# Attention scores by pairs of 64 keys, and PV on 64x32 tiles, in a fused attention and gated-FFN kernel

## The chip, the cores and the metric

One NeuronCore of a Trainium2 chip. The metric is device microseconds of one execution, the median of several. The profile is of one execution; its span runs from the first to the last instruction.

Names used below: PE is TensorE, DVE is VectorE, ACT is ScalarE, POOL is GpSimd, SP is SyncE (it issues most DMAs).

## The reference

Two layers read the same x (1 x 2048 x 512) and are mixed by a gate. A is attention in 4 segments of 512 tokens, 32 heads of 16 elements: causal softmax within the segment, plus a memory M, z that each segment reads before it adds to it. B is an FFN with 1792 hidden elements.

```python
for s in range(4):
    logits = einsum('bhqd,bhkd->bhqk', qs, ks) * scale + mask      # causal, 512 x 512
    a_dot = einsum('bhqk,bhkd->bhqd', softmax(logits), vs)
    pq = phi(qs)                                                   # x+1 if x>0 else exp(x)
    a_mem = einsum('bhld,bhde->bhle', pq, M) / (einsum('bhld,bhd->bhl', pq, z) + 1e-6)
    outs.append(g * a_mem + (1 - g) * a_dot)
    M = M + einsum('bhld,bhle->bhde', phi(ks), vs)
    z = z + phi(ks).sum(over tokens)
a = concat(outs) @ wo
b = ((x @ W_gate) * (x @ W_gate > 0) * (x @ W_up)) @ W_down
out = gate * a + (1 - gate) * b          # gate = sigmoid((x * gate_w).sum(-1))
```

All inputs and the output are bf16.

## The kernel before

**Layout.** Heads are in 4 groups G of 8. In a group, q and k lie transposed, 16 rows a head, so that a row tile of 32 partitions (there are 4, `jj`) holds two heads. PSUM is split: `psL` (4 banks) takes scores, `psA` (4 banks) everything else.

**Scores and exp.** The two heads of a row tile are told apart by masked copies of k in `kp` (L684 to L686): rows of the other head are zero. `quad` makes one load of `psL`: on each of the 4 row tiles (32x128 tiles, L765) 512 query columns against 128 keys, then one exp on ACT over 128x2048 into a slot of `E` (L773). A `full` quad takes two blocks of 128 keys of one head, from the query that is 64 past the block's first, so with widths such as 448 and 64, or 320 and 192; the triangle left in the first 64 columns of each is zeroed by an affine_select on POOL (L791). The first 64 queries of all diagonal blocks are left for `half`: one quad for two groups, 32 matmuls of 64 columns, whose 128 key rows are the first 64 keys of both heads; its masks are L809. There are 72 quads, 8 of them halves.

**PV** (`flush`) turns a group's `E` into outputs, with V and a column of ones as weights (17 columns a head). First K = 128 with 4 column tiles (128x32, L824): 32 matmuls, 2048 columns in time. Then the halves' keys on 64x32 tiles (L832), 4 column tiles in the upper and 4 in the lower 64 rows: 32 matmuls, 256 columns in time. For these, odd heads need V on the other 64 partitions: `vsh`, a DMA copy per segment (L749). Two `psA` banks are held by a visit. DVE then transposes both (L843), divides, scales by the gate (`rdg` L851, which needs `gexpT`, a DMA) and transposes to `oT`.

**Memory.** `mu` (L712) multiplies phi(k) transposed (`phik`, by DMA) with V for 128 rows and 8 heads at a time, 16 whole-array matmuls of 136 columns a segment, in two visits, for 3 segments. DVE keeps the diagonal blocks (L715), POOL adds them to `Mbd` (L717), casts to `Mbd16` (L718) and scales the ones' column (L720). `nd` reads it in the next segment (L730).

**Projections, FFN, output.** L665/L667 project q, k, v; L897 gate and up; L936 and L929 the down projection and wo, into one bank. They use the whole array (128x128).

**Order.** A planner in the kernel (`Sched`) lays out every engine's instruction stream ahead of time: it holds a cost for each operation, picks by priority among the heads of the queues (with seeded ties) and emits fixed streams with semaphore waits. PE's queues are, by priority, scores and PV, memory, projections, the output product, FFN. A quad has an earliest time, 3.2 us after the last. PV of group G is put behind the first quads of group G+1 (`gate`) and asks for free `psA` banks. Every engine works its stream in order, so that one late wait holds all that stands behind it.

Of the kernel before, what the change touches and what calls it, by code (L numbers as in the profile page):

```python
# [14 lines left out]
LAT = 60.0  # L15
PE_LAT = 175.0
# [32 lines left out]
class Epoch:  # L49
    _n = 0  # L50

    def __init__(self, cls="mid", nb=1):
        self.nb = nb
        Epoch._n += 1
        self.res = f"ACCep{Epoch._n}"
        self.bank = None
        self.readers = []
        self.cls = cls


class Op:
    __slots__ = ("engs", "eng", "fns", "occs", "lat", "reads", "writes", "name", "dma", "nbytes", "mode", "ep", "role",
                 "after", "port", "base", "preds", "stream", "idx", "start", "end", "done", "cidx", "gate", "nd")

    def __init__(self, alts, reads=(), writes=(), name="", lat=0.0, dma=False, nbytes=0, mode="f", ep=None, role=None):
# [13 lines left out]
        self.after = 0.0  # L79
        self.port = name.startswith(PORT)  # L80
# [14 lines left out]
class Sched:  # L95
# [95 lines left out]
    def pv_due(self):  # L191
        q = self.queues["pe"][self.pvq]
        while q[2] < len(q[1]) and q[1][q[2]].done:
            q[2] += 1
        if q[2] >= len(q[1]) or q[1][q[2]].gate is None:
            return False
        t = self.now["pe"] + 500.0
        return all(p.done and p.end <= t for p, _ in q[1][q[2]].preds)

    def _bank_choice(self, op, e):  # L200
        cls, nb, n = op.ep.cls, op.ep.nb, len(self.bank_ep)
        idle = [p is None or all(r.done for r in p.readers) for p in self.bank_ep]
        if cls != "att":
            held = sum(not f and p.cls == cls for f, p in zip(idle, self.bank_ep))
            if held + nb > self.CAPS.get(cls, 2) or (n - sum(idle) + nb > n - (2 if self.pv_due() else 1) if nb == 1 else sum(idle) < (2 if self.relax else 3)):
                return None
# [19 lines left out]
    def ready(self, op, e):  # L226
        t0 = self.now[e]
        t = op.after
        if op.gate is not None:
            if self.mode != "r" and not op.gate.done:  # L230
                return None
            if sum(p is None or all(r.done for r in p.readers) for p in self.bank_ep) < 2:
                return None
            t = max(t, sorted(self._bank_free(p, e) for p in self.bank_ep if p is None or all(r.done for r in p.readers))[1])
# [39 lines left out]
    def place(self, op, e, start):  # L274
        op.eng = e
        if op.ep is not None and op.role == "w" and op.ep.bank is None:
            bi, _ = self._bank_choice(op, e)
            for i in range(bi, bi + op.ep.nb):
                if self.bank_ep[i] is not None:
                    op.preds += [(r, False) for r in self.bank_ep[i].readers]  # L280
                self.bank_ep[i] = op.ep
            op.ep.bank = bi
# [122 lines left out]
def plan(S, D, F):  # L405
# [4 lines left out]
        ("qT", [128, 8, 512], BF16), ("kT", [128, 4, 512], BF16), ("kp", [128, 5, 4, 320], BF16),  # L410
# [5 lines left out]
        ("Mbd", [128, 4, 136], F32), ("Mbd16", [128, 4, 136], BF16), ("mumask", [128, 2, 136], BF16), ("mutmp", [128, 2, 136], F32),  # L416
        ("braw", [128, 32], BF16), ("eb", [128, 32], F32), ("romgh", [128, 32], F32), ("epsv", [128, 32], F32),
        ("gexp", [128, NT], F32), ("omg", [128, NT], F32), ("gexpT", [128, NT * 4], F32), ("gwb", [128, 512], BF16),  ("gl", [128, NT], F32),
        ("rden", [128, 32], F32), ("rdg", [128, 32], F32), ("rdm", [128, 128], F32), ("pm8", [128, 8], F32), ("pm", [128, 2], F32), ("pmb", [128, 64], BF16), ("ident", [128, 128], BF16),
# [3 lines left out]
def build_kernel(nc, A_x, A_wq, A_wk, A_wv, A_wo, A_beta, W_g, W_u, W_d, gate_w, out):  # L423
# [5 lines left out]
    sc = Sched(seeds=(715,715,715,5226,37223,297,89,590))  # L429
# [14 lines left out]
def program(sc, nc, T, PL, PA, A_x, A_wq, A_wk, A_wv, A_wo, A_beta, W_g, W_u, W_d, gate_w, out, NSEG, KT, NF, NT, EPS, SCALE):  # L444
# [83 lines left out]
    st = []  # L528
# [8 lines left out]
    for G in range(2):  # L537
        mv = V.mumask[:, G, :].rearrange("q (h c) -> q h c", c=17)
        st.append(pool(lambda e, mv=mv: e.tensor_copy(mv, V.pm8[:, :].unsqueeze(2).to_broadcast([128, 8, 17])), 400, reads=["pm8"], writes=[f"mumask{G}"], name="mm0"))
    st.append(pool(lambda e: e.memset(V.Mbd[:], 0.0), 700, writes=["Mbd"], name="mbd0"))  # L540
    sc.queue(1, st)
# [5 lines left out]
    ds.append(dve(lambda e: e.tensor_copy(V.pmb[:], V.pm[:, 0:1].to_broadcast([128, 64])), 220, reads=["pm"], writes=["pmb"], name="pmb"))  # L547
    sc.queue(0, ds)

# [54 lines left out]
    sc.queue(1, [t for t in cst if t.eng == "dve"])  # L604

# [47 lines left out]
    def proj(s):  # L653
# [19 lines left out]
        for G in range(4):  # L673
# [8 lines left out]
            kv = V.kT[:, G, :].rearrange("q (j k) -> q j k", j=4)  # L682
            for p, o, w in ((0, 0, 128), (1, 192, 128), (2, 128, 64)):
                km = lambda e, kv=kv, p=p, o=o, w=w, ks=ks: e.tensor_scalar(V.kp[:, ks, :, o:o + w], kv[:, :, 0:w], V.pm[:, p % 2:p % 2 + 1], None, ALU.mult)  # L684
                kq = lambda e, kv=kv, ks=ks: e.tensor_tensor(V.kp[:, ks, :, 128:192], kv[:, :, 0:64], V.pmb[:, :].unsqueeze(1).to_broadcast([128, 4, 64]), ALU.mult)
                ka = lambda e, kv=kv, p=p, o=o, w=w, ks=ks: e.activation(V.kp[:, ks, :, o:o + w], kv[:, :, 0:w], ACT.Copy, scale=V.pm[:, p % 2:p % 2 + 1])  # L686
                evs.append(sc.add(Op([("dve", km, 350 if w == 128 else 285)] + ([("act", ka, 720 if w == 128 else 500)] if s else []) + ([("pool", kq, 650)] if p == 2 and s else []), reads=[f"kT{G}", "pm"], writes=[f"kp{ks}_{p}"], name=f"kmask{s}_{G}_{p}")))
# [15 lines left out]
    def mu(s):  # L703
        pes, ds, ps = [], [], []
        for hf in range(2):
            ep = Epoch()

            def fn(e, hf=hf, ep=ep):
                for g in range(2):
                    G = 2 * hf + g  # L710
                    for tt in range(4):
                        ins = e.matmul(A(ep)[:, g * 136:(g + 1) * 136], lhsT=V.phik[:, tt, G * 128:(G + 1) * 128], rhs=V.vaug[:, s % 2, tt, 8 * G:8 * G + 8, :].rearrange("q h c -> q (h c)"), start=(tt == 0), stop=(tt == 3))  # L712
                return ins
            pes.append(pe(fn, mm(136, 8), reads=[f"phik{2 * hf}", f"phik{2 * hf + 1}"] + va(s), name=f"mu{s}_{hf}", ep=ep, role="w"))
            ds.append(dve(lambda e, ep=ep: e.tensor_tensor(V.mutmp[:, :, :], A(ep)[:, 0:272].rearrange("q (g c) -> q g c", g=2), V.mumask[:, :, :], ALU.mult), t_dve(272), reads=["mumask0", "mumask1"], writes=["mutmp"], name=f"mum{s}_{hf}", ep=ep, role="r"))  # L715
            Mh = V.Mbd[:, 2 * hf:2 * hf + 2, :]
            ps.append(pool(lambda e, Mh=Mh: e.tensor_tensor(Mh, Mh, V.mutmp[:, :, :], ALU.add), t_pool(272, 2.2), reads=["mutmp", "Mbd"], writes=["Mbd"], name=f"mua{s}_{hf}"))  # L717
        ps.append(pool(lambda e: e.tensor_copy(V.Mbd16[:], V.Mbd[:]), t_pool(544, 1.2), reads=["Mbd"], writes=["Mbd16"], name=f"mu16_{s}"))  # L718
        dc = lambda t: t[:, :, :].rearrange("q g (h c) -> q g h c", c=17)[:, :, :, 16]
        ps.append(pool(lambda e: e.tensor_tensor(dc(V.Mbd16), dc(V.Mbd), V.eb[:, :].rearrange("q (g h) -> q g h", g=4), ALU.mult), 230, reads=["Mbd", "Mbd16", "reb"], writes=["Mbd16"], name=f"mu16_{s}"))  # L720
        return pes, ds, ps

    def nd(s):
        pes, ds, sps = [], [], []
        for i in range(4):
# [9 lines left out]
            pes.append(pe(fnum, mm(136, 4), reads=[f"phiq{G}" for G in range(4)] + ["Mbd16"], name=f"num{s}_{i}", ep=ep, role="w"))  # L735
# [12 lines left out]
    def vsh_dma(s):  # L748
        Q["spv"].append(dma("sp", lambda e: e.dma_start(V.vsh[64:128, :, :, :].rearrange("q t h c -> q (t h c)"), V.vaug[0:64, s % 2, :, :, :].rearrange("q t h c -> q (t h c)")), 1 << 17, occ=700.0, reads=va(s), writes=["vsh"], name=f"vsh{s}"))  # L749
# [3 lines left out]
    def att(s, between):  # L753
        pes, acts, pools, ds, pvs = [], [], [], [], []

        def quad(tag, parts, slot=None):
            e = slot
# [4 lines left out]
            def fq(q, parts=parts):  # L762
                for (kap, _, qs, q0, o, w) in parts:
                    for jj in range(4):
                        ins = q.matmul(PL[:, jj, o:o + w], lhsT=kap(jj), rhs=V.qT[32 * jj:32 * jj + 32, qs, q0:q0 + w], start=True, stop=True, tile_position=(32 * jj, 0), skip_group_check=True)  # L765
                return ins
            rd = sorted({k for (_, ks, _, _, _, _) in parts for k in ks} | {f"qT{qs}" for (_, _, qs, _, _, _) in parts})
            np_ = len(parts)
            pes.append(pe(fq, sum(w for (_, _, _, _, _, w) in parts) / 2.4 + 10.0 + 3.0 * (np_ - 1), reads=rd, writes=[f"bankL{b}" for b in range(4)], name=f"quad{s}_{tag}", mode="r"))
            pes[-1].after = 12000.0 + 3200.0 * qctr[0]  # L770
            qctr[0] += 1
            eout = V.E[:, e, :, :] if slot is None else V.E[:, e, :, :].rearrange("q h c -> q (h c)").rearrange("q (g h c) -> q h g c", g=2, c=256)
            acts.append(act(lambda a, eout=eout: a.activation(eout, PL[:, :, :] if slot is None else PL[:, :, :].rearrange("q h (g c) -> q h g c", g=2), ACT.Exp, scale=SCALE), t_act(2048), reads=[f"bankL{b}" for b in range(4)], writes=[f"E{e}"], name=f"exp{s}_{tag}"))  # L773
            return e

        def keys(n, j):
            ks, o = kslot(s, n // 2), 192 * (n % 2)
            return lambda jj: V.kp[32 * jj:32 * jj + 32, ks, j, o:o + 128], [f"kp{ks}_{n % 2}"], qslot(s, n // 2)

        def full(tag, n, blocks):  # L780
            o, parts, regs = 0, [], []
            for j in blocks:
                w = 448 - 128 * j
                parts.append((*keys(n, j), 128 * j + 64, o, w))
                regs.append(o)
                o += w
            assert o == 512
            e = quad(tag, parts)
            for o in regs:
# [264 lines left out]
```

## Time and profile before

| | |
|---|---|
| median of 3 runs | 269.09 us (268.21 to 269.18) |
| profiled execution, span | 266.3 us |
| PE busy | 262.3 us, 2860 matmuls |
| DVE, ACT, POOL busy | 186.9, 186.8, 112.1 us |
| scores L765 | 768 matmuls, 28.7 us busy |
| PV L824 | 512 matmuls, 16.8 us busy |
| DMA | 18.13 MB, queue q1 busy 26.9% |

How to read it: a matmul's length in the trace has its drain in it, so that the lengths of one group overlap; the pace is seen from start to start. The page's rows have the line, the engine, the operation, out<-in, the shape and count; behind the bar the busy time, the mean of one in ns, and the idle time before them with what ended it. The timeline has start, length and instructions, merged where they follow each other.

### The profile page before, as it was taken

Reading aid. Unit: us, or ns where it says so; the run is one execution under the profiler, and the core shown is the slowest. Engines: PE = TensorE matmul, PEld = TensorE weight load, DVE = VectorE, ACT = ScalarE, POOL = GpSimd, SP = SyncE. Lnnn points to the kernel's source line nnn. Section 1 sums busy time; section 2 is a strip of 40 time slices with the busy share of each in tenths; the row PEclk is TensorE's granted clock in tenths of the full one; section 3 lists DMA queues with packets and bytes.
Section 4 is the critical chain, followed back from the end, with each engine's and each line's share of the span. In section 5 each row is a group of like instructions: output and inputs, shape, how many; then the busy total and the mean of one; then the engine's idle time right before and its main releaser. Section 6 shows DMA issues by size and latency. Waiting matters only on the chain.

```text
span 266.3 us, 6827 instructions
## 1 busy us (share of the span) xinstructions
PE 262.3 (98%) x2860; PEld 116.6 (44%) x2860; DVE 186.9 (70%) x370; ACT 186.8 (70%) x165; POOL 112.1 (42%) x227
## 2 busy tenths in 40 slices
PE   7999999999999999999999999999999999999996
PEld 3444444444444444444344444444444444434444
DVE  5788878888876699887868677757763556585500
ACT  3698899798896596886877687677866566774021
POOL 3025654475529343575367233822282225521000
PEclk9999999999999999999999999999999999999999
DMA  6899635921221325120022131000212000000011
GB/s 183 226 385 184 117 78 103 338 59 23 59 44 25 82 60 81 39 42 4 0 64 46 35 99 26 23 2 0 56 28 61 20 22 22 0 2 2 1 39 41
DMA packets 34209, 18.13 MB, mean 68 GB/s; under 512 B 23937, under 2 KB 33922, under 8 KB 34178
## 3 DMA queue, kind: packets, MB, share of 16 engines
q1 hardware_dynamic: 34048, 17.69, 26.9%
q8 instruction: 22, 0.36, 0.6%
q14 instruction: 9, 0.07, 0.1%
q10 hardware_dynamic: 130, 0.01, 0.0%
HBM read 9.75 MB, written 2.11 MB: 45 GB/s over the span
## 4 chain that ended last, share of the span: by engine, by line
PE 97%; DMA 1%; SPq 0%; issue 0%; ACT 0%; DVE 0%; DVEq 0%
PE psA L897 38%; PE psA L936 19%; PE psA L667 11%; PE psL L765 9%; PE psA L824 6%; PE psA L665 6%; PE psA L929 5%; PE psA L832 1%; PE psA L730 1%; PE psA L712 1%; DMA hT<-in_A_x_dram 1%; SPq L480 0%; ACT xT L578 0%; DVE osb L945 0%; PE psL L587 0%
## 5 line engine op out<-in xcount | busy, mean ns | idle before, releaser
L773 ACT ACTIVATE E<-psL 128x2048 bf16<-128x2048 f32 x72 | 135.0, 1875 | 37.7 <-PE psL L765 36.1
L791 POOL TENSOR_SCALAR_AFFINE_SELECT E<-E 128x256 bf16<-128x256 bf16 x128 | 51.8, 428 | 99.8 <-ACT E L773 91.0
L897 PE MATMUL psA<-xT,wu 128*128 128x512 bf16 x224 | 59.6, 380 | 0.0
L897 PE MATMUL psA<-xT,wg 128*128 128x512 bf16 x224 | 59.4, 380 | 0.0
L936 PE MATMUL psA<-wd,hT 128*128 128x512 bf16 (+2 forms) x238 | 54.1, 367 | 0.0
L809 POOL TENSOR_SCALAR_AFFINE_SELECT E<-E 64x512 bf16<-64x512 bf16 (+1 forms) x64 | 43.4, 703 | 23.8 <-ACT E L773 13.7
L908 DVE TENSOR_TENSOR hT<-psA,rl 128x512 bf16<-128x512 f32 x56 | 38.4, 686 | 14.6 <-PE psA L897 13.6
L843 DVE STREAM_TRANSPOSE Tn<-psA 128x512 f32<-128x512 f32 x32 | 21.2, 696 | 21.7 <-PE psA L832 21.6
L905 ACT ACTIVATE rl<-psA 128x512 bf16<-128x512 f32 x36 | 21.5, 597 | 14.9 <-PE psA L897 11.6
L897 PEld LDWEIGHTS psA<-xT,wg 128*128 128x128 bf16 x224 | 20.7, 98 | 24.8 <-issue 1.9
L936 PEld LDWEIGHTS psA<-wd,hT 128*128 128x128 bf16 x238 | 21.4, 98 | 22.7 <-issue 1.5
L897 PEld LDWEIGHTS psA<-xT,wu 128*128 128x128 bf16 x224 | 20.2, 98 | 24.2 <-issue 2.3
L765 PE MATMUL psL<-qT,kp 32*128 32x64 bf16 (+3 forms) x768 | 28.7, 245 | 0.0
L765 PEld LDWEIGHTS psL<-qT,kp 32*128 32x128 bf16 x768 | 9.9, 92 | 30.2 <-issue 18.2
L945 DVE TENSOR_SCALAR osb<-psA,omg 128x512 bf16<-128x512 f32 (+1 forms) x9 | 6.3, 695 | 16.7 <-PE psA L929 13.8
L906 DVE TENSOR_SCALAR rl<-psA 128x512 bf16<-128x512 f32 x20 | 13.8, 690 | 4.4 <-PE psA L897 3.6
L824 PE MATMUL psA<-E,vaug 128*17 128x192 bf16 (+3 forms) x512 | 16.8, 273 | 0.0
L667 PE MATMUL psA<-xT,wk 128*128 128x512 bf16 x64 | 16.6, 380 | 0.0
L667 PE MATMUL psA<-xT,wq 128*128 128x512 bf16 x64 | 16.3, 380 | 0.3 <-ACT xT L578 0.3
L929 PE MATMUL psA<-wo,oT 128*128 128x512 bf16 (+2 forms) x68 | 16.4, 367 | 0.0
L665 PE MATMUL psA<-wv,xT 128*128 128x512 bf16 x64 | 15.5, 380 | 0.0
L946 ACT ACTIVATE osb<-psA,omg 128x512 bf16<-128x512 f32 (+1 forms) x8 | 5.4, 673 | 14.0 <-PE psA L929 12.8
(82 smaller groups left out, 241.3 us busy)
## 6 DMA issues: line engine op xcount, KB each, us to landing
out_dram<-osb SPq DMA_DIRECT2D x15, 128.0 KB, 1.7
wg<-in_B_W_gate_dram SPq DMA_DIRECT2D x8, 224.0 KB, 5.4
wu<-in_B_W_up_dram SPq DMA_DIRECT2D x8, 224.0 KB, 5.6
wd<-in_B_W_down_dram SPq DMA_DIRECT2D x1, 1792.0 KB, 9.0
osb<-in_A_x_dram SPq DMA_DIRECT2D x12, 128.0 KB, 2.3
vsh<-vaug SPq DMA_DIRECT2D x4, 272.0 KB, 3.4
hT<-in_A_x_dram SPq DMA_DIRECT2D x4, 128.0 KB, 2.2
wq<-in_A_wq_dram SPq DMA_DIRECT2D x4, 128.0 KB, 2.4
```

The lines of the kernel that those rows point to most:

```text
L665: ins = e.matmul(A(ep)[:, :], lhsT=V.xT[:, kt, tok + col * 128:tok + (col + 1) * 128], rhs=w[:, kt, :], start=(kt == 0), stop=(kt == KT - 1))
L667: ins = e.matmul(A(ep)[:, :], lhsT=w[:, kt, col * 128:(col + 1) * 128], rhs=V.xT[:, kt, tok:tok + 512], start=(kt == 0), stop=(kt == KT - 1))
L765: ins = q.matmul(PL[:, jj, o:o + w], lhsT=kap(jj), rhs=V.qT[32 * jj:32 * jj + 32, qs, q0:q0 + w], start=True, stop=True, tile_position=(32 ...
L773: acts.append(act(lambda a, eout=eout: a.activation(eout, PL[:, :, :] if slot is None else PL[:, :, :].rearrange("q h (g c) -> q h g c", g ...
L791: pools.append(pool(lambda g, ap=ap: g.affine_select(out=ap, in_=ap, compare_op=ALU.is_ge, fill=0.0, base=64, pattern=[[0, 4], [1, 64]], c ...
L809: pools.append(pool(lambda e, ap=ap, base=base: e.affine_select(out=ap, in_=ap, compare_op=ALU.is_ge, fill=0.0, base=base, pattern=[[0, 8] ...
L824: ins = q.matmul(A(eps[p])[32 * jj:32 * jj + 17, 512 - w:512], lhsT=V.vaug[:, s % 2, j, 8 * G + 2 * jj + p, :], rhs=V.E[:, e, jj, o:o + w] ...
L897: ins = e.matmul(A(ep)[:, :], lhsT=w[:, kt, f * 128:(f + 1) * 128], rhs=V.xT[:, kt, c * 512:(c + 1) * 512], start=(kt == 0), stop=(kt == K ...
L905: evs.append(sc.add(Op([("act", lambda e, ep=eg, r=r: e.activation(V.rl[:, r, :], A(ep)[:, :], ACT.Relu), t_act(512)), ("dve", lambda e, e ...
L908: evs.append(dve(lambda e, ep=eu, r=r, hs=hs: e.tensor_tensor(V.hT[:, hs, :], A(ep)[:, :], V.rl[:, r, :], ALU.mult), t_dve(512), reads=[f" ...
L929: ins = e.matmul(A(ep)[:, 0:c1 - c0], lhsT=V.oT[:, o0 + G, i * 128:(i + 1) * 128], rhs=V.wo[:, G, c0:c1], start=st_ and G == 0, stop=sp_ a ...
L936: ins = e.matmul(A(ep)[:, 0:c1 - c0], lhsT=V.hT[:, slots[f], i * 128:(i + 1) * 128], rhs=V.wd[:, f, c0:c1], start=st_ and f == f0, stop=sp ...
```

## The change

- `kp` holds, for each of 8 chunks of 64 keys, those keys for head 0 and for head 1 of the row tile side by side: 128 weight columns. Two masked copies make it, not three. A quad's scores have head 0 on partitions 0 to 63 and head 1 on 64 to 127.
- Quads of a group: chunk 0 (512 queries); 1 and 7; 2 and 6; 3 and 5; and chunk 4 of two groups together. Each chunk has two masks on POOL, one of 64 and one of 128 partitions.
- PV of a group is one operation on 64x32 tiles: for 8 chunks, the upper 64 rows for head 0 and the lower for head 1, 64 matmuls of 512 to 64 columns. V is wanted on both halves, so two `vsh` copies a segment.
- The memory product is put ahead of PV of group 1 (`MU_G`), 64 products of 34 columns on 4 column tiles (128x32) into one bank; DVE adds it to `Mc`, and POOL spreads `Mc` into `Mbd16` by one masked product a group. The factor of the ones' column goes into `mumask` at the start.
- The planner counts how many free banks a PV visit asks for (`nbk`), and has other seeds, so the order of the other work moves too.

```diff
+MU_G = 1
...
-    sc = Sched(seeds=(715,715,715,5226,37223,297,89,590))
+    sc = Sched(seeds=(52936,98560,17166,30259,57195,44848,1710,92264))
...
-            kv = V.kT[:, G, :].rearrange("q (j k) -> q j k", j=4)
-            for p, o, w in ((0, 0, 128), (1, 192, 128), (2, 128, 64)):
...
+            kv = V.kT[:, G, :].rearrange("q (c k) -> q c k", c=8)
+            for p in range(2):
+                km = lambda e, kv=kv, p=p, ks=ks: e.tensor_scalar(V.kp[:, ks, :, 64 * p:64 * p + 64], kv, V.pm[:, p:p + 1], None, ALU.mult)
...
     def mu(s):
...
+        ep = Epoch("att")
+
+        def fn(e):
+            for G in range(4):
+                for tt in range(4):
+                    for j in range(4):
+                        ins = e.matmul(A(ep)[32 * j:32 * j + 32, 34 * G:34 * G + 34], lhsT=V.phik[:, tt, 128 * G + 32 * j:128 * G + 32 * j + 32],
+                                       rhs=V.vaug[:, s % 2, tt, 8 * G + 2 * j:8 * G + 2 * j + 2, :].rearrange("q h c -> q (h c)"),
+                                       start=(tt == 0), stop=(tt == 3), tile_position=(0, 32 * j), skip_group_check=True)
+            return ins
...
+        d = dve(lambda e: e.tensor_tensor(V.Mc[:], V.Mc[:], A(ep)[:, 0:136].rearrange("q (g c) -> q g c", g=4), ALU.add), t_dve(136), reads=["Mc"], writes=["Mc"], name=f"mum{s}", ep=ep, role="r")
+        ps = []
+        for G in range(4):
+            j3 = lambda t, G=G: t[:, G, :].rearrange("q (j c) -> q j c", c=34)
+            ps.append(pool(lambda e, G=G, j3=j3: e.tensor_tensor(j3(V.Mbd16), V.Mc[:, G, :].unsqueeze(1).to_broadcast([128, 4, 34]), j3(V.mumask), ALU.mult), t_pool(136, 2.2),
+                           reads=["Mc", "mumask"], writes=[f"Mbd16_{G}"], name=f"mu16_{s}"))
...
     def vsh_dma(s):
...
+        for u in range(2):
+            to, of = V.vsh[64 - 64 * u:128 - 64 * u], V.vaug[64 * u:64 * u + 64, s % 2]
...
         def quad(tag, parts, slot=None):
...
+                for G, c, o in parts:
                     for jj in range(4):
-                        ins = q.matmul(PL[:, jj, o:o + w], lhsT=kap(jj), rhs=V.qT[32 * jj:32 * jj + 32, qs, q0:q0 + w], start=True, stop=True, tile_position=(32 * jj, 0), skip_group_check=True)
+                        r = slice(32 * jj, 32 * jj + 32)
+                        ins = q.matmul(PL[:, jj, o:o + 512 - 64 * c], lhsT=V.kp[r, kslot(s, G), c, :], rhs=V.qT[r, qslot(s, G), 64 * c:512], start=True, stop=True, tile_position=(32 * jj, 0), skip_group_check=True)
...
+            o = [o for _, _, o in parts]
+            for i, x in enumerate(o):
                 for h, base in ((64, 0), (128, 64)):
+                    ap = V.E[0:h, e, :, x:x + 64]
+                    pools.append(pool(lambda g, ap=ap, base=base: g.affine_select(out=ap, in_=ap, compare_op=ALU.is_ge, fill=0.0, base=base, pattern=[[0, 4], [1, 64]], channel_multiplier=-1),
...
         def flush():
...
+            mem = mu(s) if G == MU_G and s < NSEG - 1 else None
...
+            def fpv(q):
+                for c in range(8):
+                    e, o = at[G, c]
+                    t, u = c // 2, c % 2
+                    for p in range(2):
+                        r = slice(64 * p, 64 * p + 64)
+                        v = V.vaug[r, s % 2, t, :, :] if u == p else V.vsh[r, t, :, :]
                         for jj in range(4):
-                            ins = q.matmul(A(eps[p])[32 * jj:32 * jj + 17, 512 - w:512], lhsT=V.vaug[:, s % 2, j, 8 * G + 2 * jj + p, :], rhs=V.E[:, e, jj, o:o + w],
-                                           start=(j == 0), stop=False, tile_position=(0, 32 * jj), skip_group_check=True)
...
+                            ins = q.matmul(A(eps[p])[32 * jj:32 * jj + 17, 64 * c:512], lhsT=v[:, 8 * G + 2 * jj + p, :], rhs=V.E[r, e, jj, o:o + 512 - 64 * c],
+                                           start=(c == 0), stop=(c == 7), tile_position=(64 * p, 32 * jj), skip_group_check=True)
+                return ins
...
         for G in range(4):
...
+            at |= quad(f"{G}A", [(G, 0, 0)])
+            at |= quad(f"{G}B", [(G, 1, 0), (G, 7, 448)])
             pair = flush()
...
             if G % 2 == 0:
-                half(f"{G}C", G)
+                at |= quad(f"{G}E", [(G, 4, 0), (G + 1, 4, 256)], slot=7)
+            at |= quad(f"{G}C", [(G, 2, 0), (G, 6, 384)])
             if pair:
                 pair[0].gate = pes[k]
...
+            at |= quad(f"{G}D", [(G, 3, 0), (G, 5, 320)])
```

## The prediction

> **What bounds the kernel now.** I read the page's busy shares first, then the chain that ended last, the waits of TensorE, and last the timeline of a few microseconds, where single visits can be priced.
>
> ```profile
> span 266.3 us, 6827 instructions
> PE 262.3 (98%) x2860; PEld 116.6 (44%) x2860; DVE 186.9 (70%) x370; ACT 186.8 (70%) x165; POOL 112.1 (42%) x227
> ...
> PEclk9999999999999999999999999999999999999999
> ...
> PE 97%; DMA 1%; SPq 0%; issue 0%; ACT 0%; DVE 0%; DVEq 0%
> ...
> L791 POOL TENSOR_SCALAR_AFFINE_SELECT E<-E 128x256 bf16<-128x256 bf16 x128 | 51.8, 428 | 99.8 <-ACT E L773 91.0
> ...
> L809 POOL TENSOR_SCALAR_AFFINE_SELECT E<-E 64x512 bf16<-64x512 bf16 (+1 forms) x64 | 43.4, 703 | 23.8 <-ACT E L773 13.7
> ...
> vsh<-vaug SPq DMA_DIRECT2D x4, 272.0 KB, 3.4
> ```
>
> TensorE is 98% busy, at full granted clock, and 97% of the chain. The view of its waits has three lines, all from the first microseconds:
>
> ```profile
> PE psL L553 <- PEq L1039: 0.8, 1, 0.8
> PE psA L667 <- ACT xT L578: 0.3, 1, 0.3
> PE psL L566 <- DMA hT<-in_A_x_dram: 0.2, 1, 0.2
> ```
>
> So after the start nothing holds TensorE up; its time is the sum of what it is given, and the question is what the change takes out of that sum. The timeline (start, length, instruction) prices it. A length includes the drain, so I take start to next start:
>
> ```profile
> 43.83 0.81 PE L897 MATMUL psA<-xT,wu 128*128 128x512 bf16 x3
> 44.48 0.59 PE L897 MATMUL psA<-xT,wg 128*128 128x512 bf16 x2
> 45.00 0.40 PE L765 MATMUL psL<-qT,kp 32*128 32x192 bf16 x8
> 45.33 1.05 PE L824 MATMUL psA<-E,vaug 128*17 128x448 bf16 x32
> 46.31 0.20 PE L832 MATMUL psA<-E,vaug 64*17 64x64 bf16 x4
> ...
> 46.42 0.20 PE L832 MATMUL psA<-E,vsh 64*17 64x64 bf16 x4
> 46.55 0.60 PE L897 MATMUL psA<-xT,wg 128*128 128x512 bf16 x2
> ...
> 48.82 0.41 PE L765 MATMUL psL<-qT,kp 32*128 32x64 bf16 x32
> 49.16 0.39 PE L897 MATMUL psA<-xT,wu 128*128 128x512 bf16 x1
> ```
> ```profile
> 62.14 0.64 PE L712 MATMUL psA<-vaug,phik 128*128 128x136 bf16 x8
> 62.61 1.03 PE L897 MATMUL psA<-xT,wu 128*128 128x512 bf16 x4
> ```
>
> Three 512-column matmuls take 0.65 us, 0.216 each: 0.417 ns a column and about 3 ns a matmul. A score quad (45.00 to 45.33) streams 512 columns on four row tiles, 0.213 us, and costs 0.33. The first part of PV (L824, 45.33 to 46.31) streams 2048, 0.853, and costs 0.98. Its second part (L832, to 46.55) streams 256 on eight 64x32 tiles, 0.107, and costs 0.24. Each change of tile shape therefore costs 0.12 to 0.13 us.
>
> **The change, part by part.** *PV.* Before, a visit is 0.98 + 0.24 = 1.22 us with two changes on leaving. After, it streams 512 + 448 + ... + 64 = 2304 columns on the eight tiles, as many as before (2048 + 256), and leaves once: 0.96 + 0.13 = 1.09; for the staggered start of eight chunks I take 1.10. Gain 0.12 x 16 visits = 1.9. No row shows this shape with wide streams. Bounds: 1.09 (gain 2.1), or the pace of L832 throughout: its eight groups of four start 0.11 us / 7 = 0.0157 apart, 0.031 for 64 columns, 0.49 ns a column, 1.26 a visit (loss 0.6). I take the first, because 0.031 is eight matmuls starting 4 ns apart, a charge per matmul that 512 columns cover.
>
> *Memory product.* Before: six visits like 62.14 to 62.61, 0.475 x 6 = 2.85, without a change of shape. After: three visits of 64 small products, 16 groups of four column tiles. The nearest row is again L832, where a tile gets new weights and a new product every 0.031: 16 x 0.031 = 0.50, plus 0.12 for one more change, 0.62; x 3 = 1.85. Gain 1.0. Bounds: four starts at 4 ns (0.016 a group, 0.37 a visit, gain 1.75), or each group as dear as a 136-column matmul (0.059, 1.07 a visit, loss 0.35).
>
> *Order and scores.* The instruction order has 177 changes of shape before and 165 after: 16 go with PV, 3 come with the memory product (both priced), which leaves one more, 0.12 lost. Quads stay 72 with the same columns; the eight made of 32 narrow matmuls (48.82 to 49.16, 0.34) become ordinary (0.33): 0.1 gained.
>
> Sum: 1.9 + 1.0 - 0.1 + 0.1 = 2.9 us. The profiled execution spans 266.3, the median of the runs shown is 269.09, so 2.8 lie around the span and I take the same 2.8 after: span 263.4, time **266.2**. All bounds together: 2.1 + 1.75 gives 265.2, -0.6 - 0.35 gives 270.0.
>
> The rest I cost at nothing, because it lies beside TensorE:
> - Masks. 256 of 128x256 or half as many partitions at 0.428 (L809's two forms, 64 and 128 partitions, take the same time) are 110 us where L791 and L809 take 95. GpSimd loses the third key mask (7.7 us) and the old memory update (L717, L718, L720: 7.7) and gets 12 products of 136 elements, by L717's 0.76 for 272 some 0.4 each, 5 us. In all 112 becomes about 116 of 266. A quad now ends with four masks: exp starts 0.45 after the quad, takes 1.875, masks 1.7, ready after 4.05. PV comes two or more quads later (72 quads, one in about 3.2 us), margin above 2. Thinnest is the last PV: 0.33 + 20 matmuls of 0.216 and a change are 4.75, margin 0.6. If a cover goes, all queued matmuls wait with PV.
> - The second shifted copy of V. Each PV now needs both copies at its start. In the first segment SP issues them behind the same four xT transposes, which end at 22.96, 0.6 each, and 3.4 to landing: 28. My count of the order puts the first PV at 31.6 (34.8 before). In later segments the copies wait only for the old PV, some 16 us earlier.
> - Moved on SP's queue: gscr and gexpT of segment 0 now stand behind both phik pairs and more xT transposes. From 24.2: phik 2.5, xT 1.3, phik 2.5, xT 3.9, gscr 0.5, xT 2.6, gexpT 3.1, 2.2 to landing: 42.8. On VectorE the rdg that needs it now stands behind the memory addition, which cannot run before 45. If gexpT came later than that, evictions behind rdg would stop TensorE.
> - The end. Before, the last PV's chain to oT takes 5.9 us from 244.0 with three hT products between. After, none stands between, so 3.7, under 22 matmuls, 4.75.
> - VectorE, ScalarE and GpSimd together lose 16 key masks (0.35 to 0.7 each); the four added copies (272 KB each, 1.1 MB of 18.1) fall on DMA queues that the page shows 27% busy.
>
> **Rivals.** (1) *Small products do not overlap.* If the 64 memory products each stand alone, a 34-column one is by the rows above 34 x 0.417 + 3 = 17 ns: 1.09 + 0.12 = 1.21 a visit, 3.6 in all, 0.8 lost where I count 1.0 gained: 268.0. Against it: L832 starts a matmul every 4 ns. 4%. The Trainium skill ("TensorEngine Tiling (Array Packing)", Instruction Overhead) says that each matmul pays about 60 cycles however narrow. As 64 separate charges of 25 ns, an estimate from that page, the visit would be 1.72 and the kernel 269.5; L832's 4 ns between starts on different tiles speak against such a reading, and only a charge per tile, 16 x 25 ns, is in keeping with them.
>
> (2) *PV stays at L832's pace* of 0.49 ns a column: 0.6 lost instead of 1.9 gained, 268.7. For it: it is the only row of this shape. Against: the charge looks per matmul. 7%.
>
> (3) *PV waits for masks.* A wait of 0.2 us at each of 16 visits takes 3.2 back: 269.4. For it: 192 masks become 256, and one engine makes them all. Against: 56% idle and the margins above. 7%; 3 of these go past 270.4, with 0.27 a visit.
>
> (4) *Slower: upper and lower rows do not stream side by side when wide.* Then a visit streams 4608 columns, 1.92 + 0.13 = 2.05 instead of 1.10: 15.2 more, 281.4. It decides once a visit costs over 1.37 (1.22 plus the 1.0 of the other parts and 1.35 of noise over 16). For it: no row has two wide streams there. Against: L832 passes eight 64-column streams in 0.031, where one after the other would need 0.053. 4%.
>
> **How the numbers follow.** The forecast has 78%. Faster by over 0.5% means below 267.75, slower above 270.4; half a per cent is about what a measurement of this kernel tells from no change. (1), (2) and the milder part of (3) fall between, 15%; the rest of (3), and (4), make 7%. The range goes from the best bounds, 265.2, less 0.4 for scatter (the three runs lie within 1.0), to rival (2) at 268.7: the forecast, (1) and (2) lie in it, so well over 8 in 10; the joint worst bound of 270.0 is left out.
>
> **What would show it.** PV groups of 64x32 tiles with 1.10 from first start to the next shape; memory visits of 0.5 to 0.65; changes of 0.12; waits of TensorE still only at the start; GpSimd near 116. Wrong would be: a visit of 1.26 or 2.05 (rivals 2, 4), a memory visit over 1.1 (rival 1), or a new wait of TensorE on masks, vsh or an eviction.

## The result and the profile after

| | before | after |
|---|---|---|
| median beside each other | 268.86 us (268.21 to 269.18, 4 runs) | 264.85 us (264.76 to 265.37, 4 runs) |
| profiled execution, span | 266.3 us | 263.0 us |
| matmul records, weight loads | 2860, 2860 | 2714, 2748 |
| DVE, ACT, POOL busy | 186.9, 186.8, 112.1 us | 181.5, 188.7, 119.5 us |

The ratio is 0.9866, with an interval of 0.9846 to 0.9886: 1.3% faster. The profiled execution of after took 264.76 us, 1.76 more than its span.

These lines of the page of after answer to those shown of before:

```profile
span 263.0 us, 6637 instructions
PE 254.4 (97%) x2714; PEld 113.1 (43%) x2748; DVE 181.5 (69%) x359; ACT 188.7 (72%) x167; POOL 119.5 (45%) x283
...
PEclk9999999999999999999999999999999999999999
...
PE 94%; issue 2%; DVE 1%; DMA 1%; SPq 0%; ACT 0%; DVEq 0%
...
L786 POOL TENSOR_SCALAR_AFFINE_SELECT E<-E 64x256 bf16<-64x256 bf16 (+1 forms) x256 | 111.8, 446 | 122.2 <-ACT E L781 100.9
```

TensorE is still the bound, at full granted clock. The chain has a new entry, "issue", with 2%, and the view of TensorE's waits names it too:

```profile
PE psA L874 <- issue: 2.1, 13, 0.2
PE psA L913 <- issue: 1.0, 6, 0.2
PE psL L556 <- PEq L1014: 0.8, 1, 0.8
...
PE psA L673 <- ACT xT L581: 0.3, 1, 0.3
PE psL L569 <- DMA hT<-in_A_x_dram: 0.2, 1, 0.2
```

The last three are the waits of the start, as before; behind the start TensorE waits for no mask, no copy of V and no eviction. The "issue" entries are read as no waits at all. There are 34 more weight loads than matmul records, where before had as many of each, and at 34 places two starts lie 0.22 us further apart than the pace, one 512-column matmul (0.216): a record is missing there, in 15 of them that of the first wide matmul after a PV visit. (Three of the holes are put down to DVE, 0.2 each.) Such a hole costs nothing, and the span bears that out: 34 real stops of 0.22 would be 7.5 us. The timeline (start, length, instruction) has a memory visit, then a PV visit followed by a hole:

```profile
105.64 0.66 PE L716 MATMUL psA<-vaug,phik 128*32 128x34 bf16 x64
106.23 0.39 PE L809 MATMUL psA<-E,vaug 64*17 64x512 bf16 x4
```
```profile
131.51 0.39 PE L809 MATMUL psA<-E,vaug 64*17 64x512 bf16 x4
...
132.48 0.20 PE L809 MATMUL psA<-E,vaug 64*17 64x64 bf16 x4
132.84 1.67 PE L671 MATMUL psA<-wv,xT 128*128 128x512 bf16 x7 [0.16 <-issue]
```

The memory visit takes 0.59 from its first start to PV's. From PV's first start to the next one shown is 1.33; less the missing matmul (L671 has 62 records for 64 weight loads) it is 1.11. The one visit that a quad follows, and all 16 in an experiment whose trace lacks no record (`old_memory_product`), give 1.100. All 16 visits of before take 1.22 (0.982 and 0.241), so the visits alone give 16 x 0.123 = 2.0 us.

### The profile page after: what moved, and what is told of

Its sections match the earlier page's. It is cut to its first block, busy times and chain, and to the rows that moved or that the text cites. A ratio compares the mean times of both kernels' runs of the same rounds, so it can differ in the third digit from the quotient of the medians.

```text
span 263.0 us, 6637 instructions
## 1 busy us (share of the span) xinstructions
PE 254.4 (97%) x2714; PEld 113.1 (43%) x2748; DVE 181.5 (69%) x359; ACT 188.7 (72%) x167; POOL 119.5 (45%) x283
## 4 chain that ended last, share of the span: by engine, by line
PE 94%; issue 2%; DVE 1%; DMA 1%; SPq 0%; ACT 0%; DVEq 0%
PE psA L874 37%; PE psA L913 19%; PE psA L673 11%; PE psL L775 9%; PE psA L809 7%; PE psA L906 5%; PE psA L671 5%; PE psA L736 1%; DMA hT<-in_A_x_dram 1%; PE psA L716 1%; DVE vaug L699 0%; SPq L484 0%; DVE phiq L657 0%; ACT xT L581 0%; DVE osb L922 0%
## 5 line engine op out<-in xcount | busy, mean ns | idle before, releaser
L786 POOL TENSOR_SCALAR_AFFINE_SELECT E<-E 64x256 bf16<-64x256 bf16 (+1 forms) x256 | 111.8, 446 | 122.2 <-ACT E L781 100.9
L874 PE MATMUL psA<-xT,wg 128*128 128x512 bf16 x212 | 57.0, 380 | 1.9 <-issue 1.6
L913 PE MATMUL psA<-wd,hT 128*128 128x512 bf16 (+2 forms) x229 | 52.2, 366 | 1.1 <-issue 1.0
L775 PE MATMUL psL<-qT,kp 32*128 32x192 bf16 (+7 forms) x512 | 28.5, 287 | 0.0
L882 ACT ACTIVATE rl<-psA 128x512 bf16<-128x512 f32 x32 | 19.1, 597 | 10.2 <-PE psA L874 9.5
L923 ACT ACTIVATE osb<-psA,omg 128x512 bf16<-128x512 f32 (+1 forms) x12 | 8.1, 679 | 17.9 <-PE psA L906 14.0
L883 DVE TENSOR_SCALAR rl<-psA 128x512 bf16<-128x512 f32 x24 | 16.7, 696 | 3.2 <-PE psA L874 2.5
L809 PE MATMUL psA<-E,vaug 64*17 64x128 bf16 (+7 forms) x512 | 18.7, 283 | 0.0
L809 PE MATMUL psA<-E,vsh 64*17 64x128 bf16 (+7 forms) x512 | 18.3, 283 | 0.0
L671 PE MATMUL psA<-wv,xT 128*128 128x512 bf16 x62 | 14.7, 380 | 0.3 <-issue 0.3
L809 PEld LDWEIGHTS psA<-E,vaug 64*17 64x17 bf16 x512 | 11.6, 86 | 6.0 <-issue 3.6
```

The costliest lines, as they stand in the source:

```text
L671: ins = e.matmul(A(ep)[:, :], lhsT=V.xT[:, kt, tok + col * 128:tok + (col + 1) * 128], rhs=w[:, kt, :], start=(kt == 0), stop=(kt == KT - 1))
L775: ins = q.matmul(PL[:, jj, o:o + 512 - 64 * c], lhsT=V.kp[r, kslot(s, G), c, :], rhs=V.qT[r, qslot(s, G), 64 * c:512], start=True, stop=Tr ...
L786: pools.append(pool(lambda g, ap=ap, base=base: g.affine_select(out=ap, in_=ap, compare_op=ALU.is_ge, fill=0.0, base=base, pattern=[[0, 4] ...
L809: ins = q.matmul(A(eps[p])[32 * jj:32 * jj + 17, 64 * c:512], lhsT=v[:, 8 * G + 2 * jj + p, :], rhs=V.E[r, e, jj, o:o + 512 - 64 * c], sta ...
L874: ins = e.matmul(A(ep)[:, :], lhsT=w[:, kt, f * 128:(f + 1) * 128], rhs=V.xT[:, kt, c * 512:(c + 1) * 512], start=(kt == 0), stop=(kt == K ...
L882: evs.append(sc.add(Op([("act", lambda e, ep=eg, r=r: e.activation(V.rl[:, r, :], A(ep)[:, :], ACT.Relu), t_act(512)), ("dve", lambda e, e ...
```

## The experiments

Two theories stood at the start. The first is the prediction's: PV visits shrink by 0.12, memory visits by 1.0 in all, and everything else hides beside TensorE, so that each part alone brings its own share. The rivals put the gain, or a loss that hides in it, elsewhere: in halves that do not really run together, in the order, in the masks. Each run has a time of the kernel before on the same chip: 268.46, 268.43 and 268.19 in the three batches.

### The halves of the array, one after the other: `pv_one_half_after_other`

```diff
             def fpv(q):
-                for c in range(8):
-                    e, o = at[G, c]
-                    t, u = c // 2, c % 2
-                    for p in range(2):
+                for p in range(2):
+                    for c in range(8):
+                        e, o = at[G, c]
+                        t, u = c // 2, c % 2
```

> The changed kernel with the two loops of PV swapped: all 8 chunks on the upper 64 rows, then all 8 on the lower, so that the two halves of the array no longer stream side by side. Same matmuls, same order of everything else. Theory (TensorE's time is the sum of its streams, and the gain of the new PV needs both halves at once): each visit streams 4608 columns instead of 2304, 0.96 us more, 16 visits, so 264.85 + 15.4 = 280.2, visits of about 2.06 us. Rival (the halves hardly overlap in the changed kernel either, and the gain came from elsewhere): within 3 us of the changed kernel.

Measured: 275.83 us in one run, span 274.1. A visit takes 1.81 instead of 1.10, and 16 x 0.71 = 11.4 is the span's loss of 11.1. So the gain does hang on the upper and the lower half streaming side by side. The expected loss was larger, though. The timeline of the first visit shows why:

```profile
32.40 0.28 PE L809 MATMUL psA<-E,vaug 64*17 64x256 bf16 x4
32.41 0.39 PE L809 MATMUL psA<-E,vsh 64*17 64x512 bf16 x8
32.59 0.40 PE L809 MATMUL psA<-E,vaug 64*17 64x128 bf16 x8
32.64 0.51 PE L809 MATMUL psA<-E,vsh 64*17 64x64 bf16 x8
```

In this kernel the 512-column products of the lower half come after all of the upper half's. Four of them start at 32.41, right behind the upper half's 256-column group, while the upper groups of 192, 128 and 64 columns, earlier in the program, start at 32.50, 32.59 and 32.64 (the first of them is merged into the second line). The idle half is fed about 0.24 us ahead of its turn, and a visit is 0.25 shorter than the 2.06 expected. The Trainium skill ("TensorE: Matmul & The Clock Gate", Part 3: Packing small matmuls) says that matmuls start and end strictly in program order; these starts differ from that, and the measurement decides.

### The two parts alone, with the seeds that were there

`old_memory_product` is the changed kernel with the memory product of before; `new_memory_product_alone` is the kernel before with the new memory product put ahead of PV of group 1. Neither gets new seeds.

In the first, besides `mu` and its masks as they were:

```diff
-            mem = mu(s) if G == MU_G and s < NSEG - 1 else None
+            mem = None
```

In the second, besides the new `mu` and `mumask`:

```diff
+            mem = mu(s) if G == MU_G and s < NSEG - 1 else None
+            if mem:
+                put(dmu=[mem[1]], poolmu=mem[2])
...
+            if mem:
+                pair.insert(0, mem[0])
```

> The changed kernel with the old memory product (16 whole-array matmuls of 136 columns a segment in two visits, the old update on VectorE and GpSimd), so the new scores and PV alone. Theory (sum of the parts): loses the memory part's 1.07 us (2.85 before, 3 x 0.594 after), and 2 changes of shape less than the changed kernel's 162 outside the memory visits give or take 0.1 each: 265.8 to 266.1, that is 2.8 to 3.1 under the kernel before. Rival (the smaller memory work on VectorE and GpSimd carries the gain): close to 268.9.

> The kernel before with only the memory product changed: 64 products of 34 columns ahead of PV of group 1, one bank, the new update. It stands next to PV's 128x32 part, so it has the same tile shape and costs no change of its own. Theory (sum): gains 2.85 - 3 x (0.594 - 0.10) = 1.37 us, 268.86 - 1.4 = 267.5; 177 changes of shape as before. Rival (planning for three free banks at one visit costs waits): no gain, and waits of TensorE ahead of the memory product.

Measured: 269.26 us, ratio 1.0039 (1.0027 to 1.0051), and 269.65 us, 1.0049 (1.0037 to 1.0061). Both missed: each part alone is slower than before. All PV visits of the first take 1.100, so the term is there, and something gives it back. The views of TensorE's waits, the first kernel's and then the second's:

```profile
PE psL L771 <- ACT E L777: 1.0, 1, 1.0
...
PE psA L870 <- DVE rl L879: 0.3, 1, 0.3
PE psA L902 <- DVE oT L830: 0.3, 1, 0.3
```
```profile
PE psL L773 <- ACT E L781: 1.2, 3, 0.8
...
PE psA L835 <- POOL E L799: 0.5, 1, 0.5
```

These are waits for an exp, a mask and evictions, in places where the plan has the work a little too close to its consumer. Before and after have none of them. The question became whether the parts or the order bring them.

### The seeds of before in the changed kernel: `old_seeds`

```diff
-    sc = Sched(seeds=(52936,98560,17166,30259,57195,44848,1710,92264))
+    sc = Sched(seeds=(715,715,715,5226,37223,297,89,590))
```

> The changed kernel with the planner's seeds of the kernel before, so another order of the same work; 165 changes of shape in both. Theory (TensorE's work sets the time, the order hardly matters as long as nothing waits): 264.9 to 266 , and any excess shows as waits of TensorE in the profile, not as dearer visits. Rival (the gain is that of a luckier order): 268 or more.

Measured: 274.07 us, ratio 1.0203 (1.0173 to 1.0232); the profiled span is 272.9, 9.9 over that of after. Missed widely. The waits, and the timeline at the longest of them:

```profile
PE psA L809 <- issue: 3.8, 1, 3.8
PE psL L775 <- ACT E L781: 1.7, 3, 1.0
```
```profile
50.36 0.20 PE L809 MATMUL psA<-E,vaug 64*17 64x64 bf16 x3
54.31 0.21 PE L809 MATMUL psA<-E,vaug 64*17 64x64 bf16 x1 [3.75 <-issue]
54.45 1.89 PE L874 MATMUL psA<-xT,wg 128*128 128x512 bf16 x4
```

TensorE stops between the third and the fourth matmul of a group, inside one operation, where nothing that the program waits for stands. After it, four matmuls take 1.7 us from start to start, 0.42 each, twice the usual. The view by windows (each engine's busy time; last three the granted clock, the DMA share and GB/s) confirms both:

```profile
50.40:54.30 3.90, 0.16 (x23) 0.03 (x4) 0.05 (x1) 0.00 (x0) 1.26 (x3) 0.77 1.51 343
54.30:59.30 5.00, 4.99 (x19) 1.48 (x18) 2.57 (x5) 2.42 (x2) 1.56 (x4) 0.50 0.89 92
```

The granted clock is 0.50 from 52.5 to 59.3 us, and TensorE works for 5.0 us of that, so the clock costs 2.5. With the stop of 3.8 and the other waits (1.7 for exps, some 1.2 more) that is 9.2 of the 9.9; the rest is not placed. Since the program has no wait inside an operation, the cause of the stop is to be looked for outside it. The trace has a DMA queue of instructions (q8, 16 KB each, one for some 260 of TensorE's records). In this kernel none of its packets runs between 34.9 and 51.5 us, with DMA at 343 GB/s from the loads of `wo` and `wd` at the end of that time; then one comes, and 2.8 us after its start TensorE resumes. In after the fetch starts at 46.2, just as those loads are issued.

### The same with the load of `wd` later: `old_seeds_late_wd`

```diff
     for t in lsp:
         t.after = 42000.0
+    lsp[-1].after = 52000.0
```

> The changed kernel with the old seeds, where TensorE stopped for 3.9 us inside a PV visit at 50.4 us and then ran 4 us at half clock, now with the 1.8 MB load of wd planned 10 us later; the order of TensorE is the same up to 60 us. Theory (the stop is an instruction fetch that stood behind that load: the fetch queue moved nothing from 33.7 to 51.5 us): no stop at 50 us, and 272 falls to 266 to 268, unless a later fetch meets the load instead. Rival (the stop has to do with the PV visit itself): it stays at 50 us.

Measured: 269.57 us, ratio 1.0046 (1.0033 to 1.0058). The stop is at the same instruction and now 1.3 us long; the granted clock stays at 1.00:

```profile
50.07 0.20 PE L810 MATMUL psA<-E,vaug 64*17 64x64 bf16 x3
51.40 0.19 PE L810 MATMUL psA<-E,vaug 64*17 64x64 bf16 x1 [1.13 <-issue]
```

The fetch comes at 49.0, behind `wo` alone, instead of 51.5, and TensorE resumes 2.4 us after its start. So moving 1.8 MB of loading out of the way cuts the stop by 2.5 us, keeps the clock and takes 4.5 us off the kernel: that this load lengthens the stop is shown. The stop did stay at 50 us, as the rival said, but the rival doesn't explain why its length follows the load. That the fetch is the link, and that `wo` makes the 1.3 us that are left, is read from the records; no run moved the fetch itself or `wo`. The time misses what was expected by these 1.3 us and by waits of 0.9, 0.7 and 0.5 at other places.

### The two parts alone, each with an order of its own

The same two kernels again, with seeds for which the planner's own plan leaves little of TensorE idle.

```diff
-    sc = Sched(seeds=(52936,98560,17166,30259,57195,44848,1710,92264))
+    sc = Sched(seeds=(72224,66228,45311,67877,42182,25599,42182,67877))
```
```diff
-    sc = Sched(seeds=(715,715,715,5226,37223,297,89,590))
+    sc = Sched(seeds=(71326,715,4683,6717,55110,55110,92428,590))
```

> The run with the old memory product again, with other planner seeds, found for this kernel so that the plan has little idle TensorE time. In the first such run TensorE waited about 2.6 us that the changed kernel does not wait. Theory (sum of the parts, and waits are a matter of the order): its matmuls and changes of shape come to 1.2 us more than the changed kernel's, so 264.85 + 1.2 = 266.0 and up to 266.6 with small waits, 2 to 2.5 under the kernel before (268.46 in the same batch). Rival (the new PV alone gains nothing, it needs the new memory product beside it): 268 or more.

> The run with the memory product alone changed again, with planner seeds found for it. Theory: 1.4 us less work for TensorE than the kernel before, so 268.46 - 1.4 = 267.1, to 267.6 with small waits. Rival (three banks at one visit cost waits whatever the order): 268.5 or more, with waits ahead of the visits of group 1.

Measured: 266.45 us, 0.9922 (0.9900 to 0.9943), and 267.33 us, 0.9956 (0.9939 to 0.9972). The first has no wait of TensorE behind the start, the second 0.6 us of them by the starts (the view of waits names 0.2). So the new scores and PV bring 268.43 - 266.45 = 2.0 us, the new memory product 1.1, and the two losses above were the order's. In the second kernel the memory visit needs no change of shape of its own, so that 1.4 was to be had, less those waits; in after it is 1.07. The sum of 3.1 stands against a gain of both of 3.3 in the profiled spans and 4.0 in the medians, or 3.6 against the median of before in the next batch (268.46).

### Masks: `masks_twice` and `masks_one_and_a_half`

The first makes every mask twice, in the same order; the second only those of 128 partitions.

```diff
+                        if op.name.startswith("mask"):
+                            op.fns[e](engobj).then_inc(self.sem["again"], 1)
+                            extra += 1
+                            engobj.wait_ge(self.sem["again"], extra)
                         res = op.fns[e](engobj)
```

In the second the condition is:

```diff
-                        if op.name.startswith("mask"):
+                        if op.name.startswith("mask") and "m64" in op.writes[0]:
```

> The changed kernel, every instruction in its order, but GpSimd makes each mask twice (same result): 256 masks become 512, busy 119.5 + 112 = 231 us, 88% of the span. Theory (the cover of the masks is 2 us or more at all PV visits and 0.6 at the last): after a quad with two chunks the masks end 0.45 + 1.9 + 3.6 = 5.9 us after its start; PV two quads later, 6.4, does not wait; only the last one, 4.75 after, waits 1.2: 264.85 + 1.2 = 266.0. Rival (the masks are nearly on the path already): waits at most of the 16 visits, 270 or more.

> The changed kernel, same order, with only the second mask of each chunk (128 partitions) made twice: 384 masks instead of 256, the same 3 for every 2. With 512 masks TensorE waited for masks at 15 places, up to 3.5 us: a quad with two chunks then brought 8 masks of 0.448, 3.6 us, and quads come every 3.2 us, so that GpSimd fell behind. Theory now (the cover is a rate): 6 masks are 2.7 us a quad, under 3.2, so no backlog; the last PV, 4.75 after its quad, waits 0.45 + 1.9 + 2.7 - 4.75 = 0.3: 265 to 266. Rival (GpSimd is already at its limit in the changed kernel, where 4 masks are 1.8): one half of the loss of the doubled run, 275 or more.

Measured: 300.41 us, ratio 1.1207 (1.1173 to 1.1242), missed by far; and 265.18 us, 0.9895 (0.9878 to 0.9913), as expected. The waits of TensorE on masks, first and second:

```profile
PE psA L814 <- POOL E L791: 21.1, 13, 3.5
PE psA L721 <- POOL E L791: 3.5, 2, 2.5
```
```profile
PE psA L814 <- POOL E L791: 0.4, 1, 0.4
```

A quad with twice its four masks needs 8 x 0.448 = 3.6 us of POOL, and a quad comes every 3.2: a backlog grows, and 13 PV visits wait for it, and two memory visits that stand directly in front of a PV: 15 of 16 places. (The rest of the loss is clock: five times it is halved for 3.41 us, of which TensorE works 16.4 in all, so 8.2 us are lost.) The view by windows shows when it is halved. The first window here has a part of the longest wait (3.46 us, from 67.07 to 70.53), the second a wait of 2.1 us, the third is what follows that. After the window stand its length and PE's busy time; the last three figures are as above.

```profile
65.46:68.87 3.41, 1.61 (x14) 0.51 (x12) 1.87 (x4) 3.41 (x4) 3.14 (x7) 1.00 0.19 51
...
273.67:277.08 3.41, 1.36 (x7) 0.39 (x5) 0.69 (x1) 0.00 (x0) 2.90 (x8) 1.00 0.01 2
277.08:280.50 3.42, 3.37 (x68) 1.68 (x69) 1.18 (x2) 0.00 (x0) 0.00 (x0) 0.50 0.02 5
```

The changes of the clock in this trace lie whole multiples of 3.41 us apart, and the windows are such steps. Where TensorE was busy for 0.5 to 1.4 us of a step, the clock was halved in the next; where it was busy for 1.6 or more, it was not. The longest wait falls into two steps and costs no clock.

Half as many extra masks, six or 2.7 us a quad, leave POOL ahead: it is busy 67%, and only the last PV waits, because behind the last exp it has no slack.

### Fewer weight columns in the memory product: `memory_half_weights`

```diff
-    ins = e.matmul(A(ep)[32 * j:32 * j + 32, 34 * G:34 * G + 34], lhsT=V.phik[:, tt, 128 * G + 32 * j:128 * G + 32 * j + 32],
+    ins = e.matmul(A(ep)[32 * j:32 * j + 16, 34 * G:34 * G + 34], lhsT=V.phik[:, tt, 128 * G + 32 * j:128 * G + 32 * j + 16],
```

> The changed kernel, same order, with memory products whose weights are 16 columns instead of 32 (it leaves out the odd heads' part of the memory). In the changed kernel the first 28 products of a visit start about 3.6 ns apart (25 ns for each four) and the rest 8.3 ns apart (33 ns for each four). Supply theory (each product is a weight load and a matmul, and TensorE's stream brings one of the two about every 4.15 ns once what it had queued is used up): nothing changes, visits of 0.59. Weight theory (the time is that of loading 32 columns): the later products come closer, visits of 0.53 or less. The kernel's time is the same within 0.2 us in both.

Measured: 265.13 us in one run; a visit takes 0.58 instead of 0.59. In both, groups of four products start 25 ns apart at first and 33 ns apart from the ninth group on, with 8 ns from each product to the next. Half the weight columns leave both paces as they are, so the width of the weights doesn't set them. That how fast loads and products are handed over sets them is the theory that is left; no run tests it further.

## Why the prediction was right

**PV.** Predicted 1.10 a visit, measured 1.100: the wide streams keep the 0.417 ns a column of the whole array, and one change of shape falls away. Rival 2 (0.49 a column) is out, as the choice said: the 4 ns between starts is a charge per matmul that wide streams cover. Rival 4 is out as well: what it feared happens only if the halves are given their work one after the other, and costs 0.71 a visit then. Rival 3 is out too, since TensorE waits for no mask. `old_memory_product_ordered` gives 2.0 for PV and scores, by the steps 1.9 + 0.1.

**Memory product.** Predicted 0.62 a visit, measured 0.59: 2.85 less 3 x 0.594 is 1.07 instead of 1.0. Rival 1 (1.21 a visit) is out. The row that was used, a tile with new weights every 31 ns, was the right neighbour (25 to 33 ns).

**Order and scores.** Shape changes went from 177 to 165, as counted.

**The sum.** 2.9 was predicted for the span, 3.3 came. The memory product gives 0.08 of the difference. Another 0.27 is two small holes of before, 0.11 us at 36.9 and 0.16 at 129.0 between starts, too short for the view of waits, that the new order doesn't have. Counting starts against the known paces would have found them.

**Around the span: the term that was mis-sized.** The prediction took 2.8 us from the difference between the median of before (269.09) and the span of one profiled execution (266.3), and carried it over. Seventeen executions of before in the first batch give spans of 266.2 to 266.9 with times of 267.96 to 268.70: 1.7 to 1.8 lies around each, as in after (1.76). So the profiled execution had taken about 268.05, an estimate, and the other 1.0 was that the median stood above it. With 1.75 the same steps give 263.4 + 1.75 = 265.15, against the 264.85 measured. The time forecast was 1.35 high, 1.0 of it by this term and 0.4 by the span. The steps inside the span were right, but that the time still lies in the stated range is luck: the range's lower end, 264.8, is only 0.05 below the result, and it lies there because 0.4 had been taken off for scatter.

**What was costed at nothing.** All of it held. GpSimd came to 119.5 where 116 was counted: a mask takes 446 ns in the mean, not 428, and the memory's products 479, not 400. The `vsh` copies of the first segment were issued at 22.92 (predicted 22.96). On SP's queue gscr was issued at 37.5 and gexpT through to 42.6, some 2 us later than counted, mostly because a pair of phik transposes took 4.0 there and not 2.5, and the two copies ahead of it 1.9 and not 1.2; nothing waited for it, since rdg first runs at 46.2. At the end the last mask was ready 0.68 us ahead of the last PV (0.6 predicted), and its chain to oT took 4.0 us (246.14 to 250.14), not 3.7; wo's product started at 251.0.

**What the reasoning lacked.** Two of its steps gave a right number for an incomplete reason. It put the cover of the masks as a lead of more than 2 us over PV. That lead is worth something only while POOL makes a quad's masks faster than quads come: at 2.7 us a quad all but the last PV stay covered, at 3.6 one of 16 does. And it looked for the change's other effects on particular queues, taking for granted that the rest of the order would be as good. Three runs say that this is not free: with seeds that were not made for it, the same work takes 2.3 us (`new_memory_product_alone`) or 2.8 us (`old_memory_product`) longer than with seeds found for it, and 9.2 us longer than after in `old_seeds`, where the stop and the clock behind it make 6.3 in the profiled execution. The gain is that of the parts, not of the seeds, since before itself had only 0.27 us of waits behind the start to lose; but it shows only in an order that hides the rest. The forecast had no rival with a bad order in it, and the chance of one could not have been read from the profile of before.

No version that combines anything beyond the changed kernel was run; a search for an order with one change of shape fewer would be worth 0.1 us by the rows, less than these runs resolve.

## What to carry to other kernels

On an engine that is busy all the time, price a change by starts, not lengths: columns times the pace, plus changes of tile shape (0.12 us here), and take what lies around the span from executions whose time and span are both known. Small tiles cost no more than large ones when all of the array has a stream at the same time and the streams are long against a start (4 ns); give the halves their work alternately. When work moves to a helper engine, compare its time per round with the round's length first, and only then its lead; and test a part of a planned kernel alone only with a plan made for it.

## What the runs showed of the hardware

- TensorE can stop in the middle of an operation while large loads run: for 3.8 us with 2.3 MB of loads ahead of an instruction fetch, for 1.3 us with 0.5 MB. That the fetch is what it waits for is read from the records, not shown. The view of waits calls it "issue", like a missing record; a true stop is told by its length, which need not be that of one matmul, and by TensorE, VectorE and ScalarE all falling idle (GpSimd does so once its queued masks are done).
- The granted clock fell to 0.50 at 52.51, some 2 us into the stop of 3.8, and stayed there until 59.34, two steps of 3.41 us; after the stop of 1.3 it stayed 1.00. The Trainium skill ("TensorE: Matmul & The Clock Gate", Part 1: The HAM clock gate) states that the clock is halved after an idle window of about 3.4 us. The length of the step agrees with that, but no idle time of 3.4 us is needed here: in `masks_twice` waits of 2.1 to 3.3 us halved the clock five times, and one of 3.46 did not. In both traces together it was halved behind steps with 0.5 to 1.46 us of work and kept at full behind steps with 1.61 or more; at half, a step with 1.61 did not bring it back and one with 2.92 did.
- In `pv_one_half_after_other`, products for an idle half of the array start ahead of earlier ones that wait for the other half (32.41 against 32.50 to 32.64).
- A run of small products on changing tiles starts one group of four every 25 ns, and every 33 ns from the ninth group on.
